# Cutting GpSimd's attention multiplies into four pieces, and a shorter run of rank operations

## The chip, the cores and the metric

The kernel runs on one core of a Trainium2 chip, in one launch. The metric is the device time of one execution in microseconds (us), the median of the runs. Engines are called as in the profile: PE (TensorE), DVE (VectorE), ACT (ScalarE), POOL (GpSimd), SP (the queue that issues most DMAs).

## The reference, cut to what matters

```python
kv  = einsum('bhsd,bhse->bhde', k, v)              # 4 batches, 8 heads, 576 positions, 64 wide
out = einsum('bhsd,bhde->bhse', q, kv)
out = out / sqrt(mean(out*out, -1) + 1e-6) * g_norm
x   = out.transpose(0, 2, 1, 3).reshape(2304, 512)  # 2304 tokens = 18 tiles of 128
# first mixture: tokens with x @ w_skip > 0 go to expert argmax(x @ w_gate), 8 experts, 512->1024->512
y   = gate * (relu(x @ w1[e]) @ w2[e]);  x[chosen] += y
# second mixture: all tokens, other weights, capacity 576 an expert
out[i] = gate * (relu(x[i] @ w1[e]) @ w2[e])
```

## The kernel before, in words

**Attention.** Tokens are worked off in 18 tiles of 128 (`emit_tile`, L734). For a tile PE multiplies q with the batch's kv matrix into PSUM (`emit_products`, L730); the same product carries 34 more columns per head pair, from which the tile's 17 logits come. ACT squares the result (L739), DVE sums the squares per head (L741), ACT copies the result out of PSUM as `og` (L747; DVE does so for tile 15) and takes the root (L749), DVE takes its reciprocal `ri` (L751) and forms the logits in `Lall` (L755, L757). POOL then does two multiplies over 128 x 512 elements at L762: `og` by the norm weights, in place, and `xr` = `og` by `ri`. SP stores `xr` to the token table `xcat` in HBM (L765), one DMA a tile, in SP's order.

**Routing.** While the tiles run, the chosen experts are made into one-hots and ranks in two parts, tiles 0 to 8 and tiles 9 to 17. `onehot_all` (L148) is six DVE operations over (tiles x 8 experts). `rank_part` (L167) makes running counts `C` on DVE (L173), lets PE sum them over partitions (L178 to L183), and turns ranks `rk` into a block number `hb` (L200, L202), a place in the block `a` (L204), block one-hots `os` (L207), their product with the experts `Bt` (L214), and per tile a 128 x 128 one-hot `As` of the place (L218), all on DVE. PE multiplies `As` with `Bt` (L794, L855), which gives each slot's token number. In the second part the total of the counts, `sum`, is one small POOL addition (L188); PE's matmul L260 in `order_experts` takes `sum`, and its result is what DVE sorts the experts by. The call for the first mixture has two blocks (`nb` = 2), that for the second three.

**An early start.** After the first part the largest expert is known. Its first 128 tokens are gathered by POOL (`gather`, L339) as soon as their numbers are there (`tokens`, L271 to L273), and SP loads its weights (L329). PE starts on them (L574, L592) while the second part of the routing is finished.

**What sets the order.** PE's order is written out by hand in `ATT_SEQ` and `EARLY_SEQ`; the part of it around the change is "v7 t v3 h0 h1 R h2 h3 T y0 y1": fill-in matmuls, transposes `t` of the gathered rows, the hidden blocks `h0`, `h1`, then `R` (the rank matmuls L178 to L183 and L260), `h2`, `h3`, then `T` (L855). DVE, ACT, POOL and SP run their instructions in the order that a planner gave them, by priority (the program's order, with `late` parts behind) and by its own costs; each engine then runs strictly in that order. POOL's order in this stretch is: the multiplies of the tiles, the gather in the midst of them, and last the copy of the one-hots (L677) and `sum` (L188).

Of the kernel before, what the change touches and what calls it, by code (L numbers as in the profile page):

```python
# [11 lines left out]
ALU = mybir.AluOpType  # L12
# [5 lines left out]
B, H, S, HD = 4, 8, 576, 64  # L18
# [13 lines left out]
EPS_G = 1e-9  # L32
LPOOL = 16
G_DVE = (15,)
EARLY_SEQ = "v7 t v3 h0 h1 R h2 h3 T y0 y1"
ATT_SEQ = ["t0 c0 c1 t1 t2 c2 c3 c4 t3 T", "t0 c0 c1 t1 t2 c2 c3 c4 t3 T t4", "r t0 q c0 c1 t1 t2 c2 c3 R c4 t3 T", "e m0 m1 E w w p0 p1 t2 w w t3 t4"]
KV_COL = True
# [5 lines left out]
def blocks(n):  # L43
    return [(r, min(128, n - r)) for r in range(0, n, 128)]
# [3 lines left out]
def moe_kernel(ctx: ExitStack, tc: tile.TileContext, qT, kk, vv, aux, w1a, w2a, w1b, w2b, capacity, out):  # L48
    nc = tc.nc
# [29 lines left out]
    pi100 = cst.tile([128, NT, 2], F32, name="pi100")  # L79
# [63 lines left out]
    def behind(inst, other):  # L143

        tc.add_manual_dep(inst.ins, other.ins.name, mybir.DependencyInfo(mybir.DependencyClass.NoSync, mybir.DependencyReason.SCHED_ONLY),
                          reason="what waits for other comes first")
# [17 lines left out]
    ahead = {}  # L164
    As = rt.tile([128, NT, 128], BF16, name="As")

    def rank_part(st, ohv, i0, i1, ps_pool, tag, base=None, bump=None):  # L167

        m, nb = st["m"], st["nb"]
        n = i1 - i0  # L170
        nm = lambda s: f"{s}_{m}_{i0}"
        C = rt.tile([128, E, n], BF16, name=nm("C"))
        nc.vector.tensor_tensor_scan(out=C.rearrange("p e i -> p (e i)"), data0=smask[n].rearrange("p e i -> p (e i)"),  # L173
                                     data1=ohv.rearrange("p e i -> p (e i)"), initial=0.0, op0=ALU.mult, op1=ALU.add)
        yield
        R = ps_pool.tile([128, E, n], F32, name=tag)
        prev = st["sum"]
        nc.tensor.matmul(R, lhsT=ones, rhs=C, start=True, stop=False)  # L178
        if prev is not None:
            nc.tensor.matmul(R, lhsT=ones, rhs=prev.unsqueeze(2).to_broadcast([128, E, n]), start=False, stop=False)  # L180
        if bump is not None:
            nc.tensor.matmul(R, lhsT=identb, rhs=bump.unsqueeze(2).to_broadcast([128, E, n]), start=False, stop=False)
        nc.tensor.matmul(R, lhsT=ntri, rhs=ohv, start=False, stop=True)  # L183
        if prev is None:
            st["sum"] = C[:, :, n - 1]
        else:
            st["sum"] = rt.tile([128, E], BF16, name=nm("sum"))
            ins = nc.gpsimd.tensor_tensor(out=st["sum"], in0=prev, in1=C[:, :, n - 1], op=ALU.add)  # L188
            if m == 1 and bump is not None:
                behind(ins, ahead["gather"])  # L190
        if i1 == NT and m == 1:
            order_experts(st, ps_pool, tag)
        rk8 = rt.tile([128, E, n], F32, name=nm("rk8"))
        if base is not None:
            nc.vector.tensor_tensor(out=rk8, in0=R, in1=base.unsqueeze(2).to_broadcast([128, E, n]), op=ALU.add)
        nc.vector.tensor_tensor(out=rk8, in0=R if base is None else rk8, in1=ohv, op=ALU.mult)
        rk = rt.tile([128, n], F32, name=nm("rk"))
        nc.vector.tensor_reduce(out=rk, in_=rk8.rearrange("p e i -> p i e"), axis=AX.X, op=ALU.add)
        hb = rt.tile([128, n], F32, name=nm("hb"))
        nc.vector.tensor_scalar(out=hb, in0=rk, scalar1=128.0, scalar2=None, op0=ALU.is_ge)  # L200
        for k in range(2, nb + 1):
            nc.vector.scalar_tensor_tensor(out=hb, in0=rk, scalar=128.0 * k, in1=hb, op0=ALU.is_ge, op1=ALU.add)  # L202
        a = rt.tile([128, n], F32, name=nm("a"))
        nc.vector.scalar_tensor_tensor(out=a, in0=hb, scalar=-128.0, in1=rk, op0=ALU.mult, op1=ALU.add)  # L204
        os_ = rt.tile([128, n, 2, nb], BF16, name=nm("os"))
        for k in range(nb):
            nc.vector.scalar_tensor_tensor(out=os_[:, :, :, k], in0=hb.unsqueeze(2).to_broadcast([128, n, 2]), scalar=float(k),  # L207
                                           in1=pi100[:, i0:i1, :], op0=ALU.is_equal, op1=ALU.mult)
        x2 = 2 * nb
        Bt = st["Bt"]  # L210
        step = 6 if n == NT else n
        for h0 in range(0, n, step):
            hs = slice(h0, h0 + step)
            nc.vector.tensor_tensor(out=Bt[:, i0 + h0:i0 + h0 + step], in0=ohv[:, :, hs].rearrange("p e i -> p i e").unsqueeze(3).to_broadcast([128, step, E, x2]),  # L214
                                    in1=os_[:, hs].rearrange("p i q b -> p i (q b)").unsqueeze(2).to_broadcast([128, step, E, x2]), op=ALU.mult)
            for i in range(h0, h0 + step):
                eng = nc.gpsimd if m == 1 and i1 == NT and i < AS_POOL else nc.vector
                eng.tensor_scalar(out=As[:, i0 + i, :], in0=rowb, scalar1=a[:, i:i + 1], scalar2=None, op0=ALU.is_equal)  # L218
# [37 lines left out]
    def order_experts(st, ps_pool, tag):  # L256

        m = st["m"]
        cps = ps_pool.tile([128, E], F32, name=tag)
        nc.tensor.matmul(cps, lhsT=ones, rhs=st["sum"], start=True, stop=True)  # L260
        key = rt.tile([128, E], F32, name=f"key_{m}")
        nc.vector.tensor_tensor(out=key, in0=cps, in1=st["head"], op=ALU.add)
        sort_experts(st, key)
        cnt0 = rt.tile([1, E], F32, name=f"cnt0_{m}")
        nc.scalar.copy(out=cnt0, in_=cps[0:1])
        st.update(ends=cnt0)
# [370 lines left out]
    with att:  # L637
# [96 lines left out]
        def emit_tile(i):  # L734
            if i not in PS:
                emit_products(i)
            ps, t0 = PS[i], i * 128
            sq = asp.tile([128, 4, 128], F32, name="sq")
            nc.scalar.activation(out=sq, in_=ps[:, :, 0:128], func=AF.Square)  # L739
            ss = asp.tile([128, H], F32, name="ss")  # L740
            nc.vector.tensor_reduce(out=ss, in_=sq.rearrange("p c (h d) -> p (c h) d", h=2), axis=AX.X, op=ALU.add)  # L741
            og = aog.tile([128, H, HD], F32, name="og")
            o4, og4 = ps[:, :, 0:128].rearrange("p c (h d) -> p c h d", h=2), og.rearrange("p (c h) d -> p c h d", c=4)
            if i in G_DVE:
                nc.vector.tensor_tensor(out=og4, in0=o4, in1=grep.unsqueeze(1).unsqueeze(1).to_broadcast([128, 4, 2, HD]), op=ALU.mult)
            else:
                nc.scalar.copy(out=og4, in_=o4)  # L747
            rm = asp.tile([128, H], F32, name="rm")
            nc.scalar.activation(out=rm, in_=ss, func=AF.Sqrt, bias=eps6, scale=1.0 / HD)  # L749
            ri = asp.tile([128, H], F32, name="ri")  # L750
            nc.vector.reciprocal(out=ri, in_=rm)  # L751
            xr = axp.tile([128, ROW], F32, name="xr")
            r4 = ri.rearrange("p (c h) -> p c h", c=4).unsqueeze(3)
            lh = asp.tile([128, 4, 2, 17], F32, name="lh")
            nc.vector.tensor_tensor(out=lh, in0=ps[:, :, 128:162].rearrange("p c (h n) -> p c h n", h=2),  # L755
                                    in1=r4.to_broadcast([128, 4, 2, 17]), op=ALU.mult)
            nc.vector.tensor_reduce(out=Lall[:, i, :], in_=lh.rearrange("p c h n -> p n (c h)"), axis=AX.X, op=ALU.add)  # L757
            (nc.gpsimd.tensor_copy if i >= LPOOL else nc.scalar.copy)(out=xr[:, D:ROW], in_=Lall[:, i, 0:16])
            steps = [] if i in G_DVE else [(og, grep.unsqueeze(1))]
            steps.append((xr[:, 0:D].rearrange("p (h d) -> p h d", h=H), ri.unsqueeze(2)))  # L760
            for k, (dst, by) in enumerate(steps):
                ins = nc.gpsimd.tensor_tensor(out=dst, in0=og, in1=by.to_broadcast([128, H, HD]), op=ALU.mult)  # L762
                if "gather" in ahead and k == 0 and i > ahead["first"]:
                    behind(ins, ahead["gather"])
            nc.sync.dma_start(out=xcat[t0:t0 + 128, :], in_=xr)  # L765

        with tc.manual_schedule(engines={mybir.EngineType.PE}):
# [74 lines left out]
            with tc.tile_pool(name="e1t", bufs=2, space=PSUM, reuse_waits="tile") as p1t, \  # L842
                    tc.tile_pool(name="e1h", bufs=2, space=PSUM, reuse_waits="tile") as p1h, \
                    tc.tile_pool(name="e1y", bufs=2, space=PSUM, reuse_waits="tile") as p1y:
                for u in EARLY_SEQ.split():
                    if u == "t":
# [22 lines left out]
    with first_mix:  # L869
# [288 lines left out]
        step = tc.manual_schedule(engines={mybir.EngineType.PE})  # L1158
# [100 lines left out]
    with tc.tile_pool(name="m2y", bufs=1) as m2y, tc.tile_pool(name="m2o", bufs=4) as m2o, \  # L1259
# [85 lines left out]
        for p, j in enumerate(ORDER2):  # L1345
# [16 lines left out]
            nb = len(blocks(CAP2[j]))  # L1362
# [61 lines left out]
```

## Time and profile before

| | us |
|---|---|
| runs: median (lowest to highest of 3) | 495.9 (495.35 to 496.73) |
| the profiled execution, its own time | 496.99 |
| its span in the trace | 495.3 |

The span is the time from the first to the last instruction of the trace; the profiled execution took 1.7 us more than its span, which lies around it. In the rows below, times are us from the span's start, durations us unless marked ns. "L762" is line 762 of the program. In a timeline row the first number is the start, the second the duration (of several instructions together where "x2" stands), and in brackets the idle time of the engine just before and what ended it.

### The profile page before, as it was taken

How to read it: one execution, taken by the hardware profiler on the slowest of the kernel's cores; microseconds unless marked ns; L12 is line 12 of the kernel's file. 1: busy time of each engine (PE TensorE's matmuls, PEld its weight loads, DVE VectorE, ACT ScalarE, POOL GpSimd, SP SyncE). 2: the span in 40 equal slices, each digit the busy share in tenths (PEclk: the TensorE clock that was granted, in tenths of full speed). 3: DMA queues.
4: the chain of work that ended last, by engine and by line, in shares of the span. 5: the costliest groups of instructions: out<-in, count | busy, mean ns of one | idle time of the engine just before them, and what ended most of it. 6: DMA issues, size and time to landing. Idle time of an engine off the chain costs nothing.

```text
span 495.3 us, 10229 instructions
## 1 busy us (share of the span) xinstructions
PE 472.4 (95%) x3829; PEld 450.1 (91%) x3829; DVE 303.6 (61%) x942; ACT 205.3 (41%) x524; POOL 146.5 (30%) x179
## 2 busy tenths in 40 slices
PE   6998689999999999999998999999999999999995
PEld 3897578999999999999897899999999999999984
DVE  2157988568766775356774576565657566675711
ACT  1376451354352532106143364454545545555400
POOL 5288684104112032022123240220604124040201
PEclk9599999999999999999999999999999999999999
DMA  8999495998868676259119983554656656300001
GB/s 244 367 360 343 166 356 145 359 357 313 293 216 284 228 246 235 97 195 346 60 47 343 396 293 140 201 189 154 212 185 221 204 174 216 148 37 1 36 23 41
DMA packets 24617, 104.90 MB, mean 212 GB/s; under 512 B 3609, under 2 KB 4761, under 8 KB 15984
## 3 DMA queue, kind: packets, MB, share of 16 engines
q1 hardware_dynamic: 17264, 77.75, 45.6%
q0 software_dynamic: 7008, 26.35, 15.2%
q8 instruction: 32, 0.52, 0.4%
q14 instruction: 25, 0.20, 0.1%
q10 hardware_dynamic: 288, 0.07, 0.1%
HBM read 92.15 MB, written 12.76 MB: 212 GB/s over the span
## 4 chain that ended last, share of the span: by engine, by line
PE 75%; DVE 4%; DMA 2%; issue 1%; ACT 0%; POOL 0%; POOLq 0%; ACTq 0%
PE hp L592 14%; PE yp L1086 7%; PE yp L1088 7%; PE yp L1087 7%; PE hp L1086 6%; PE yp L616 6%; PE hp L1087 6%; PE hp L1088 6%; PE yp L626 5%; PE yp L617 2%; PE yt L1317 2%; DMA wraw<-in_w1b 2%; PE tp L1273 2%; PE tp L1010 1%; PE tp L574 1%; DVE wlo L979 1%
## 5 line engine op out<-in xcount | busy, mean ns | idle before, releaser
L978 ACT CAST whi<-wraw 128x512 fp32r<-128x512 f32 x152 | 86.1, 619 | 75.0 <-PE yp L1087 30.1
L979 DVE TENSOR_TENSOR wlo<-wraw,whi 128x512 fp32r<-128x512 f32 x152 | 97.3, 685 | 28.9 <-ACT whi L978 27.8
L339 POOL DMA_INDIRECT rows<-xcat,gi x40 | 42.6, 1064 | 137.3 <-ACT ex L348 86.0
L1086 PE MATMUL hp<-xh,whi 128*128 128x256 f32 (+7 forms) x256 | 78.9, 308 | 0.2 <-DVE hl L1106 0.2
L592 PE MATMUL hp<-xT,wraw 128*128 128x128 f32 (+8 forms) x576 | 78.0, 292 | 0.3 <-issue 0.3
L1088 PE MATMUL hp<-xh,wlo 128*128 128x256 f32 (+7 forms) x256 | 76.6, 299 | 0.0
L1087 PE MATMUL hp<-xl,whi 128*128 128x256 f32 (+7 forms) x256 | 76.6, 299 | 0.0
L592 PEld LDWEIGHTS hp<-xT,wraw 128*128 128x128 f32 x576 | 73.4, 190 | 2.5 <-issue 2.4
L1307 POOL DMA_INDIRECT out<-ot,toki x24 | 34.6, 1444 | 85.4 <-DVE su L352 39.4
L1086 PE MATMUL yp<-hh,whi 128*128 128x320 f32 (+5 forms) x192 | 58.8, 306 | 0.0
L1087 PE MATMUL yp<-hl,whi 128*128 128x320 f32 (+5 forms) x192 | 57.3, 298 | 0.0
L1088 PE MATMUL yp<-hh,wlo 128*128 128x320 f32 (+5 forms) x192 | 57.2, 298 | 0.0
L1086 PEld LDWEIGHTS hp<-xh,whi 128*128 128x128 f32 x256 | 48.2, 188 | 1.0 <-DVE hl L1106 0.7
L1087 PEld LDWEIGHTS hp<-xl,whi 128*128 128x128 f32 x256 | 48.4, 189 | 0.0
L1088 PEld LDWEIGHTS hp<-xh,wlo 128*128 128x128 f32 x256 | 48.2, 188 | 0.0
L1026 POOL DMA_INDIRECT xcat<-rows,toki x16 | 16.4, 1026 | 92.5 <-DVE mxt L297 90.0
L616 PE MATMUL yp<-hT,whi 128*128 128x352 f32 (+4 forms) x160 | 43.1, 351 | 0.0
L1105 ACT ACTIVATE hh<-hp 128x320 fp32r<-128x320 f32 (+8 forms) x64 | 27.2, 429 | 32.2 <-PE hp L1088 27.4
L1106 DVE SCALAR_TENSOR_TENSOR hl<-hp,hh 128x320 fp32r<-128x320 f32 (+8 forms) x64 | 30.1, 477 | 13.5 <-ACT hh L1105 12.3
L617 PE MATMUL yp<-hT,wlo 128*128 128x176 f32 (+4 forms) x160 | 37.8, 236 | 0.0
L1087 PEld LDWEIGHTS yp<-hl,whi 128*128 128x128 f32 x192 | 36.2, 188 | 0.0
L1086 PEld LDWEIGHTS yp<-hh,whi 128*128 128x128 f32 x192 | 36.1, 188 | 0.0
(253 smaller groups left out, 866.6 us busy)
## 6 DMA issues: line engine op xcount, KB each, us to landing
wraw<-in_w1a SPq DMA_DIRECT2D x14, 1024.0 KB
wraw<-in_w2a SPq DMA_DIRECT2D x14, 1024.0 KB
wraw<-in_w1b SPq DMA_DIRECT2D x14, 1024.0 KB
wraw<-in_w2b SPq DMA_DIRECT2D x14, 1024.0 KB
xcat<-xr SPq DMA_DIRECT2D x18, 264.0 KB
q<-in_q SPq DMA_DIRECT2D x3, 1152.0 KB
wraw<-in_k SPq DMA_DIRECT2D x6, 512.0 KB
wraw<-in_v SPq DMA_DIRECT2D x6, 512.0 KB
```

The costliest lines, as they stand in the source:

```text
L339: return nc.gpsimd.indirect_dma_start(out=rows[:n], out_offset=None, in_=xcat[0:source], in_offset=bass.IndirectOffsetOnAxis(ap=gi[:n], ax ...
L592: nc.tensor.matmul(hp[:, ff, :], lhsT=wv[:, fc % 4, k, :], rhs=XT[j][:, k, c0:c1], start=(k == 0), stop=(k == 3))
L616: nc.tensor.matmul(yp, lhsT=wh[:, fc, :], rhs=HT[j][:, fc], start=(fc == 0), stop=False, skip_group_check=True)
L617: nc.tensor.matmul(yp[:, 0, :], lhsT=wl[:, fc, :], rhs=HT[j][:, fc, 0, :], start=False, stop=(fc == 7), skip_group_check=True)
L978: nc.scalar.copy(out=hi[:, cs], in_=raw[:, cs])
L979: ins = nc.vector.tensor_tensor(out=lo[:, cs], in0=raw[:, cs], in1=hi[:, cs].bitcast(F32), op=ALU.subtract)
L1086: nc.tensor.matmul(ps, lhsT=wh, rhs=xh, start=first, stop=False)
L1087: nc.tensor.matmul(ps, lhsT=wh, rhs=xl, start=False, stop=False)
L1088: nc.tensor.matmul(ps, lhsT=wl, rhs=xh, start=False, stop=last)
L1105: ea = nc.scalar.activation(out=hh[:, fs, cs], in_=hp, func=AF.Relu)
L1106: ev = nc.vector.scalar_tensor_tensor(out=hl[:, fs, cs], in0=hp, scalar=0.0, in1=hh[:, fs, cs].bitcast(F32), op0=ALU.max, op1=ALU.subtract)
L1307: st = nc.gpsimd.indirect_dma_start(out=out, out_offset=bass.IndirectOffsetOnAxis(ap=r2["toki"][:nn, j, bi:bi + 1], axis=0), in_=ot[:nn], ...
```

## The change

From tile 7 on (the eighth) each POOL multiply of 128 x 512 elements is issued as four instructions of 128 x 128, two heads each. In `rank_part`, with two blocks, `hb` becomes minus 128 or 0 in one operation, `a` is the sum of `hb` and `rk`, and the two `os` one-hots compare `rk` with 128 directly: four DVE operations where there were five, and `os` no longer reads `hb`. With three blocks nothing changes. `rank_part` runs with two blocks twice.

```diff
+PIECES = (7, 4)
...
-        nc.vector.tensor_scalar(out=hb, in0=rk, scalar1=128.0, scalar2=None, op0=ALU.is_ge)
-        for k in range(2, nb + 1):
-            nc.vector.scalar_tensor_tensor(out=hb, in0=rk, scalar=128.0 * k, in1=hb, op0=ALU.is_ge, op1=ALU.add)
...
-        nc.vector.scalar_tensor_tensor(out=a, in0=hb, scalar=-128.0, in1=rk, op0=ALU.mult, op1=ALU.add)
...
-        for k in range(nb):
-            nc.vector.scalar_tensor_tensor(out=os_[:, :, :, k], in0=hb.unsqueeze(2).to_broadcast([128, n, 2]), scalar=float(k),
-                                           in1=pi100[:, i0:i1, :], op0=ALU.is_equal, op1=ALU.mult)
+        if nb == 2:
+            nc.vector.tensor_scalar(out=hb, in0=rk, scalar1=128.0, scalar2=-128.0, op0=ALU.is_ge, op1=ALU.mult)
+            nc.vector.tensor_tensor(out=a, in0=hb, in1=rk, op=ALU.add)
+            for k, op in enumerate((ALU.is_lt, ALU.is_ge)):
+                nc.vector.scalar_tensor_tensor(out=os_[:, :, :, k], in0=rk.unsqueeze(2).to_broadcast([128, n, 2]), scalar=128.0,
+                                               in1=pi100[:, i0:i1, :], op0=op, op1=ALU.mult)
+        else:
...
             for k, (dst, by) in enumerate(steps):
-                ins = nc.gpsimd.tensor_tensor(out=dst, in0=og, in1=by.to_broadcast([128, H, HD]), op=ALU.mult)
-                if "gather" in ahead and k == 0 and i > ahead["first"]:
-                    behind(ins, ahead["gather"])
+                by = by.to_broadcast([128, H, HD])
+                step = H if i < PIECES[0] else H // PIECES[1]
+                for h0 in range(0, H, step):
+                    hs = slice(h0, h0 + step)
+                    ins = nc.gpsimd.tensor_tensor(out=dst[:, hs], in0=og[:, hs], in1=by[:, hs], op=ALU.mult)
+                    if "gather" in ahead and k == 0 and i > ahead["first"]:
+                        behind(ins, ahead["gather"])
```

## Rows read from the trace of the kernel before

**Rows 1.** The page: busy time of the engines over the span.

```profile
PE 472.4 (95%) x3829; PEld 450.1 (91%) x3829; DVE 303.6 (61%) x942; ACT 205.3 (41%) x524; POOL 146.5 (30%) x179
```

**Rows 2.** The chain of waits, 0 to 95 us, first piece: start, us, what.

```profile
82.41 0.34 issue
```

**Rows 3.** The timeline of PE, 48 to 78 us.

```profile
48.09 0.19 PE L178 MATMUL lg<-C,ones 128*128 128x72 bf16 x1 [1.80 <-DVE C L173]
...
59.73 0.35 PE L794 MATMUL acc<-Bt,As 128*128 128x32 bf16 x2 [1.31 <-DVE As L218]
...
68.41 0.63 PE L574 MATMUL tp<-ident,rows 128*128 128x128 f32 x4 [1.74 <-DMA rows<-xcat,gi]
...
73.72 0.18 PE L260 MATMUL lg<-sum,ones 128*128 128x8 bf16 x1 [0.33 <-DVE rk L196]
73.82 3.81 PE L592 MATMUL hp<-xT,wraw 128*128 128x128 f32 x32
```

**Rows 4.** Stretches: length, PE, PEld, DVE, ACT, POOL busy; PE clock; DMA.

```profile
39.70:72.90 33.20, 25.73 (x236) 22.39 (x235) 29.83 (x89) 18.14 (x50) 26.08 (x28) 0.95 0.81 283
44.30:62.00 17.70, 12.07 (x123) 10.56 (x122) 17.38 (x58) 8.56 (x24) 11.65 (x12) 0.96 0.65 225
56.00:60.00 4.00, 1.01 (x11) 0.56 (x9) 4.00 (x17) 2.12 (x6) 2.30 (x2) 1.00 0.17 68
61.00:63.00 2.00, 2.00 (x9) 2.00 (x9) 1.94 (x7) 0.20 (x1) 1.50 (x2) 0.50 0.97 377
```

**Rows 5.** DVE, single lines: duration ns least/median/most, first and last start.

```profile
L157 DVE TENSOR_TENSOR oa_eq<-Lall,oa_mx x3: 309/630/968, 44.7 to 81.5; 128x72 f32<-128x72 f32 x2, 128x144 f32<-128x144 f32 x1
...
L200 DVE TENSOR_SCALAR hb<-rk x3: 168/171/1033, 50.8 to 92.5; 128x9 f32<-128x9 f32 x2, 128x18 f32<-128x18 f32 x1
...
L202 DVE SCALAR_TENSOR_TENSOR hb<-rk,hb x4: 160/178/961, 51.8 to 92.9; 128x9 f32<-128x9 f32 x2, 128x18 f32<-128x18 f32 x2
...
L204 DVE SCALAR_TENSOR_TENSOR a<-hb,rk x3: 160/178/1191, 52.8 to 93.1; 128x9 f32<-128x9 f32 x2, 128x18 f32<-128x18 f32 x1
...
L533 DVE TENSOR_SCALAR lead_1l<-key_1l,mx_1l x1: 890/890/890, 56.4 to 56.4; 128x8 f32<-128x8 f32 x1
...
L218 DVE TENSOR_SCALAR As<-rowb,a x36: 232/251/916, 54.1 to 97.4; 128x128 bf16<-128x128 bf16 x36
...
L271 DVE SCALAR_TENSOR_TENSOR tok<-tab x6: 159/162/940, 60.9 to 255.6; 128x1 f32<-128x1 f32 x3, 128x14 f32<-128x14 f32 x1, 128x2 f32<-128x2 f32 x1, 128x21 f32<-128x21 f32 x1
```

**Rows 6.** The timeline of POOL, 0 to 73 us.

```profile
2.00 0.58 POOL L100 MEMSET capc<- 1x1 f32 x16
...
8.57 4.08 POOL L964 TENSOR_SCALAR inslot<-pcol 128x1 f32<-128x1 f32 x16
...
39.70 1.26 POOL L762 TENSOR_TENSOR og<-og,au 128x512 f32<-128x512 f32 x1
...
42.07 2.49 POOL L762 TENSOR_TENSOR og<-og,au 128x512 f32<-128x512 f32 x2
44.52 2.05 POOL L762 TENSOR_TENSOR xr<-og,ri 128x512 f32<-128x512 f32 x2
...
60.76 1.04 POOL L762 TENSOR_TENSOR xr<-og,ri 128x512 f32<-128x512 f32 x1 [1.13 <-issue]
62.30 1.29 POOL L339 DMA_INDIRECT rows<-xcat,gi  x1 [0.50 <-DVE gi L272]
...
70.42 0.20 POOL L758 COPY xr<-Lall 128x16 f32<-128x16 f32 x1
70.59 1.03 POOL L762 TENSOR_TENSOR xr<-og,ri 128x512 f32<-128x512 f32 x1
...
72.65 0.21 POOL L188 TENSOR_TENSOR sum<-C,C 128x8 bf16<-128x8 bf16 x1
```

**Rows 7.** The timeline of SP's queue, 51 to 60 us.

```profile
51.81 6.37 SPq L765 DMA_DIRECT2D xcat<-xr  x3
59.05 0.90 SPq L329 DMA_DIRECT2D wraw<-in_w1a  x2
```

More of the change, by code (lines that the diff above doesn't have):

```diff
@@ L199, in rank_part @@
         hb = rt.tile([128, n], F32, name=nm("hb"))
-        nc.vector.tensor_scalar(out=hb, in0=rk, scalar1=128.0, scalar2=None, op0=ALU.is_ge)
-        for k in range(2, nb + 1):
-            nc.vector.scalar_tensor_tensor(out=hb, in0=rk, scalar=128.0 * k, in1=hb, op0=ALU.is_ge, op1=ALU.add)
         a = rt.tile([128, n], F32, name=nm("a"))
-        nc.vector.scalar_tensor_tensor(out=a, in0=hb, scalar=-128.0, in1=rk, op0=ALU.mult, op1=ALU.add)
         os_ = rt.tile([128, n, 2, nb], BF16, name=nm("os"))
-        for k in range(nb):
-            nc.vector.scalar_tensor_tensor(out=os_[:, :, :, k], in0=hb.unsqueeze(2).to_broadcast([128, n, 2]), scalar=float(k),
-                                           in1=pi100[:, i0:i1, :], op0=ALU.is_equal, op1=ALU.mult)
+        if nb == 2:
[5 more added lines that the diff above has]
+        else:
+            nc.vector.tensor_scalar(out=hb, in0=rk, scalar1=128.0, scalar2=None, op0=ALU.is_ge)
+            for k in range(2, nb + 1):
+                nc.vector.scalar_tensor_tensor(out=hb, in0=rk, scalar=128.0 * k, in1=hb, op0=ALU.is_ge, op1=ALU.add)
+            nc.vector.scalar_tensor_tensor(out=a, in0=hb, scalar=-128.0, in1=rk, op0=ALU.mult, op1=ALU.add)
+            for k in range(nb):
+                nc.vector.scalar_tensor_tensor(out=os_[:, :, :, k], in0=hb.unsqueeze(2).to_broadcast([128, n, 2]), scalar=float(k),
+                                               in1=pi100[:, i0:i1, :], op0=ALU.is_equal, op1=ALU.mult)
         x2 = 2 * nb
```

## The prediction

> **What bounds the kernel now.** I read the page first: PE is busy 95% of the span [rows 1], so any time that PE loses comes out at the end. The chain of waits, read from its start, begins only at 82.41 us [rows 2]; from there on it is nearly all PE, so what a change before 82 us is worth is how much earlier or later PE gets there, and the timeline of PE between 48 and 78 us is the view that decides. It shows four waits: 1.80 us for the counts `C` of DVE, 1.31 us for `As` of DVE, 1.74 us for the gathered rows, 0.33 us ahead of L260 [rows 3]. From L260 at 73.72 us on PE has matmuls back to back until the chain of waits takes over [rows 3].
>
> The first three waits lead to DVE: of the 17.70 us from 44.3 to 62.0 it is busy 17.38 [rows 4], and the gather at 62.30 waits for its `gi` [rows 6]. DVE is slow there because it meets POOL. The first L157 starts at 44.7 and takes 0.97 us, ending at 45.66; the first of two `xr` multiplies that start at 44.52 ends half-way through their 2.05 us, at 45.55 [rows 5, 6]. With POOL idle the same operation on twice the elements takes 0.31 [rows 5]. So a DVE operation that reads two operands from SBUF, or a small tensor_scalar, stands until the POOL multiply that it met is over, and gets in ahead of the next one. POOL itself is busy 26.08 of the 33.20 us from 39.7, where tile 7's multiplies start, to 72.9, just behind `sum` (72.65 + 0.21 = 72.86) [rows 4, 6]: 7.1 us idle.
>
> **The change part by part. DVE's gain.** Eight stalls on DVE's way to the gather, long minus short duration [rows 5]: L157 and the operation after it, 0.97 - 0.23 each (0.23 is an estimate from half of 0.31 and the fixed part of the others): 1.48; L200 1.03 - 0.17: 0.86; L202, which goes: 0.96; L204 1.19 - 0.16: 1.03; L533 0.89 - 0.17 (L200's short form stands in): 0.72; the worst `As` 0.92 - 0.25: 0.67; L271 0.94 - 0.16: 0.78. Sum 6.5 us. With pieces, the seven that stay still wait for a piece, at most 0.42 us long (below); I take half, 0.2 each: 1.4 back. POOL will also have few gaps left, so the operations that fell into its gaps until now (two `os`, `Bt`, half of the nine `As`, three small ones of the lead expert, some 11) wait 0.2 us each: 2.2 back. Net 6.5 - 1.4 - 2.2 = 2.9 us; bounds 6.5 (no waits left) and 6.5 - 18 x 0.42 = -1.1. The dropped operation of the second `rank_part` saves 0.16 us [rows 5], ahead of `T`, which PE reaches behind h3 in any case: nothing.
>
> **POOL's price.** 21 multiplies (10 by the norm weights, since tile 15's is on DVE, and 11 by `ri`) become 84. No row before shows a 128 x 128 multiply on POOL, so I work it out from starts, not durations. A multiply by the weights takes 1.26 us alone and two take 2.49, so one follows another after 1.23; by `ri` 2.05 - 1.04 = 1.01 [rows 6]. Their small end: `sum`, the same operation on 8 elements, takes 0.21, and with the 0.03 by which neighbours overlap that is 0.17 to 0.18; the copy of 16 elements at 70.42 is followed at 70.59, after 0.17 [rows 6]. Through 0.17 at 8 and 1.23 at 512 elements a straight line gives 0.42 at 128, four of them 1.69: +0.46. By `ri`: 0.37, four 1.48: +0.47. Sum 10 x 0.46 + 11 x 0.47 = 9.8 us. From both sides: a fixed part f costs 63 f. The cheapest small row is the memset, 0.58/16 = 0.036 (2.3 us in all), the dearest the tensor_scalar, 4.08/16 = 0.255 (16.1 us) [rows 6]. I take f of some 0.155, that of the same operation and of the copy, which agree.
>
> POOL's order puts `sum` behind all of these multiplies, and they start at 39.70 as before, since the work up to there is untouched. DVE running earlier can only take out POOL's idle time, 7.1 us. So `sum` ends no sooner than 72.86 + 9.8 - 7.1 = 75.6. L260 needs it, and PE is in order: behind L260 stand h2, h3, `T` and all that follows. L260 then starts at about 75.7 instead of 73.72: **+2.0 us**. The early gather lies in POOL's order behind tile 13's `xr`, 14 multiplies into the stretch: 39.70 + 7 x (1.69 + 1.48) + 0.35 for the one-hot copy = 62.2, about its 62.30 of now, so DVE's gain doesn't reach the rows either; if the planner puts the gather ahead of tile 13's pieces, h0 and h1 start earlier and PE only waits longer at L260. Two further steps lie beside this wait. SP's weight loads at 59.05 stand behind the store of tile 12 [rows 7]; with POOL behind, that `xr` ends at 39.70 + 6 x 3.17 + 0.35 = 59.1 and the loads go out about a microsecond later, so h0 and h1 end about 74.3, still ahead of 75.7. From L260 on everything moves together (the sort on DVE waits for its result as PE's h2 does), and nothing behind it makes up for the loss, PE being the chain. The added instructions wait for `og` as one did, and DVE delaying single pieces, at 0 to 1.5 us in all, is left to the range.
>
> The profiled execution took 496.99 us, 1.1 above the median of the runs: its span 495.3 + 1.7. With +2.0 it would take 499.0, and the median 495.9 + 2.0 = **497.9**.
>
> The rows put f at 0.155 from two places. [...]
>
> **The rivals.** (a) Pieces are cheap, and DVE's gain passes. With f up to 0.08 the added 5.0 us stay within the 7.1 idle plus the 0.75 us that `sum` has in hand at L260 (73.72 - 72.86, less 0.1 for the signal), the gather comes 2.9 us sooner, and so do the rows, `C`, `sum` and L260: 495.9 - 2.9 = 493.0. For it: DVE has no other slack in the stretch; against it: POOL's small instructions, none of which but the memset starts its follower in under 0.17. It decides from f = 0.125 downwards (7.85/63). (b) The two cancel: f between 0.10 and 0.15, L260 within 1.5 us of now: 495.9. [...] (d) The dearer fixed part, 0.2: 12.6 added, 500.7.
>
> **How the numbers follow.** Forecast 0.44, with 496.4 to 500.0 as its own range (f from 0.13 to 0.19); (a) 0.27; (b) 0.15; (c) 0.09; (d) 0.05. 0.3%, 1.5 us, is about what a measurement of this kernel can tell from no change. Faster by more: (a) nearly whole, 0.26. Within: (b) and the lower end of the forecast, 0.24. Slower by more: 0.50. The range from 493.0 to 500.5 leaves the better half of (a) below and (d) above, 0.17 in all.
>
> **What the profile after would show.** Right: `og` and `xr` pieces follow one another after 0.37 to 0.43 us, POOL has almost no idle time from 39.7 to the gather and on to `sum`, `sum` ends at 75 us or later, PE idles ahead of L260 with POOL as what ended it, and no DVE operation there takes over 0.6 us. Wrong: pieces 0.35 us apart or less, `sum` done well ahead of h1's end, the gather before 60. My figures fall if the planner puts `sum` ahead of the last pieces, or if POOL's idle time can't be used because pieces wait for ACT; then only the first half, DVE's gain, or only the second is seen.

## The result and the profile after

The changed kernel takes 500.44 us (median of four runs, 500.04 to 503.38) against 495.75 for the kernel before in the same comparison: 4.7 us longer by the medians; over all runs the ratio is 1.0105, with a 95% interval of 1.0063 to 1.0146. The forecast was 497.9, so the sign was right and the size was not. The profiled execution took 500.69 us with a span of 499.0, 3.7 us more than before. Line numbers have moved by 1 to 12: L158 is the comparison that was L157, L774 the multiplies, L179 the rank matmuls, L268 the matmul that takes `sum`.

The page, busy time of each engine: POOL has 63 instructions and 8.9 us more [rows 1], DVE two instructions fewer and yet 4.6 us more.

```profile
PE 474.8 (95%) x3824; PEld 452.6 (91%) x3829; DVE 308.2 (62%) x940; ACT 205.4 (41%) x524; POOL 155.4 (31%) x242
```

The timeline of PE (start, duration, and in brackets the idle time before it with what ended it):

```profile
50.99 0.22 PE L179 MATMUL lg<-C,ones 128*128 128x72 bf16 x1 [4.51 <-DVE C L174]
...
71.40 1.09 PE L582 MATMUL tp<-ident,rows 128*128 128x128 f32 x4 [4.24 <-DMA rows<-xcat,gi]
...
73.56 4.13 PE L600 MATMUL hp<-xT,wraw 128*128 128x128 f32 x32
78.48 0.21 PE L179 MATMUL lg<-C,ones 128*128 128x72 bf16 x1 [0.79 <-DVE C L174]
79.11 0.18 PE L268 MATMUL lg<-sum,ones 128*128 128x8 bf16 x1 [0.33 <-DVE rk L197]
```

The wait for `C` has grown from 1.80 to 4.51 us, that for the rows from 1.74 to 4.24, and L268 starts 5.39 us later than L260 did [rows 3]. `C` comes from DVE, and the rows come late because POOL, which issues their gather, had stood for DVE before. DVE's timeline shows why:

```profile
44.59 0.37 DVE L765 TENSOR_REDUCE Lall<-lh 128x17 f32<-128x136 f32 x1
44.88 4.41 DVE L158 TENSOR_TENSOR oa_eq<-Lall,oa_mx 128x72 f32<-128x72 f32 x1
49.33 0.23 DVE L159 TENSOR_TENSOR oa_eq<-oa_eq,w 128x72 f32<-128x72 f32 x1
...
53.76 0.81 DVE L207 SCALAR_TENSOR_TENSOR os<-rk,pi 128x18 bf16<-128x18 f32 x2
54.49 0.43 DVE L205 TENSOR_TENSOR a<-hb,rk 128x9 f32<-128x9 f32 x1
...
70.33 6.43 DVE L158 TENSOR_TENSOR oa_eq<-Lall,oa_mx 128x72 f32<-128x72 f32 x1
76.80 0.23 DVE L159 TENSOR_TENSOR oa_eq<-oa_eq,w 128x72 f32<-128x72 f32 x1
```

The first comparison of each part, over 128 x 72 elements, takes 4.41 and 6.43 us; before it took 0.97 and 0.63 [rows 5]. At 53.76 and 54.49, `os` and `a` take some 0.4 us each: these got in at the end of a piece, as forecast. POOL's timeline shows what the comparisons stood for:

```profile
39.90 1.69 POOL L774 TENSOR_TENSOR og<-og,au 128x128 f32<-128x128 f32 x4
41.55 1.47 POOL L774 TENSOR_TENSOR xr<-og,ri 128x128 f32<-128x128 f32 x4
42.99 2.52 POOL L774 TENSOR_TENSOR og<-og,au 128x128 f32<-128x128 f32 x6
...
47.73 1.46 POOL L774 TENSOR_TENSOR xr<-og,ri 128x128 f32<-128x128 f32 x4
50.66 0.33 POOL L685 COPY OH<-oh 128x72 bf16<-128x72 bf16 x1 [1.47 <-DVE oh L162]
...
75.21 1.46 POOL L774 TENSOR_TENSOR xr<-og,ri 128x128 f32<-128x128 f32 x4
76.63 0.19 POOL L766 COPY xr<-Lall 128x16 f32<-128x16 f32 x1
78.14 0.33 POOL L685 COPY OH<-oh 128x72 bf16<-128x72 bf16 x1 [1.32 <-DVE oh L162]
78.50 0.21 POOL L189 TENSOR_TENSOR sum<-C,C 128x8 bf16<-128x8 bf16 x1
```

The first comparison ends at 49.29; POOL's last piece ahead of the copy of `OH` ended at 47.73 + 1.46 = 49.19. The second ends at 76.76; POOL's last piece ends at 75.21 + 1.46 = 76.67. So neither comparison stood for one piece. Each stood until POOL stopped, and POOL stopped only because its next instruction, the copy, needs the one-hots that hang on this very comparison: POOL then waits 1.47 and 1.32 us for DVE, on top.

### The profile page after: what moved, and what is told of

It is laid out like the page before. It is cut to its first block, busy times and chain, and to the rows that moved or that the text cites. A ratio compares the mean times of both kernels' runs of the same rounds, so it can differ in the third digit from the quotient of the medians.

```text
span 499.0 us, 10286 instructions
## 1 busy us (share of the span) xinstructions
PE 474.8 (95%) x3824; PEld 452.6 (91%) x3829; DVE 308.2 (62%) x940; ACT 205.4 (41%) x524; POOL 155.4 (31%) x242
## 4 chain that ended last, share of the span: by engine, by line
PE 77%; DVE 3%; DMA 1%; issue 0%; ACT 0%; POOL 0%; POOLq 0%; ACTq 0%
PE hp L600 14%; PE yp L1098 7%; PE yp L1100 7%; PE yp L1099 7%; PE hp L1098 6%; PE hp L1099 6%; PE hp L1100 6%; PE yp L624 6%; PE yp L634 5%; PE yp L625 2%; PE tp L1285 2%; PE yt L1329 2%; PE tp L1022 1%; PE tp L582 1%; DMA rows<-xcat,gi 1%; PE lg L1009 1%
```

## The experiments

The question is why a comparison of DVE stands behind a whole run of POOL's pieces while `os` and `a` stand behind one. Theories A and B are told in the first expectation. Times are compared with the kernel before on the same chip.

**The stall by itself.** A kernel with none of the computation, executed once: 23 stretches of POOL multiplies, most of them 20 of 128 x 128, and beside each stretch one DVE operation run twice, in other sizes and forms.

```diff
+        for c in range(count):
...
+            ins = nc.gpsimd.tensor_tensor(out=d, in0=s, in1=b.to_broadcast([128, h, 64]), op=ALU.mult)
...
+        go = nc.vector.tensor_reduce(out=st, in_=flag, axis=AX.X, op=ALU.max)
...
+        for z in "xy":
...
+            ins = test(r)
```

> This kernel leaves the whole computation out: POOL runs stretches of back-to-back multiplies (mostly 20 of 128x128 f32, some of 256, 512 and 64 columns, two with a memset after each), and in each stretch DVE runs one two-input or tensor_scalar operation twice. Theory A (a DVE operation of the kind of the first one-hot comparison, 72 f32 elements with one operand repeated along the row, is not let in between 128-column pieces and stands until POOL pauses): that form takes over 5 us, until its stretch of some 8 us ends, while 9 or 18 elements take 0.2 to 0.5 us. Which of size, operand order, repeated operand or number type decides shows from the forms beside it. Rival B (it is let in at the next piece's end, as the prediction had it, and the 4.4 and 6.4 us in the changed kernel had another cause): every form takes 0.2 to 0.6 us with 128-column pieces, and up to 1.4 us with 512 columns.

No multiply of a stretch depends on another; `test` is the DVE operation. Its groups for one form, a DVE multiply over 9, 18, 36, 72 and 144 elements, the first run of each (least/median/most duration in ns, then start):

```profile
L81 DVE TENSOR_TENSOR rdax<-big x1: 437/437/437, 4.9 to 4.9; 128x9 f32<-128x9 f32 x1
...
L81 DVE TENSOR_TENSOR rdbx<-big x1: 8149/8149/8149, 12.9 to 12.9; 128x18 f32<-128x18 f32 x1
...
L81 DVE TENSOR_TENSOR rdcx<-big x1: 354/354/354, 21.5 to 21.5; 128x36 f32<-128x36 f32 x1
...
L81 DVE TENSOR_TENSOR rddx<-big x1: 8203/8203/8203, 29.9 to 29.9; 128x72 f32<-128x72 f32 x1
...
L81 DVE TENSOR_TENSOR rdex<-big x1: 467/467/467, 38.6 to 38.6; 128x144 f32<-128x144 f32 x1
```

Neither theory survives: 18 and 72 elements stand 8.2 us, to the end of the stretch ("locked"), and 9, 36 and 144 do not ("open"). The same alternation goes on through the other forms of 128 columns, up to the stretch of 256. What alternates is POOL's history. After a stretch in which DVE was locked out, POOL's next instruction had to wait for it (0.2 us ahead of the stretch with 36 elements, 0.3 ahead of that with 144), and the stretch behind this pause was open. There DVE got through early, POOL ran into the next stretch without a pause, and that one was locked. Hence theory A2: after an unbroken run of POOL instructions DVE is no longer let in at their ends, until POOL pauses.

Two of the last stretches don't fit A2 as it stands. That of 64 columns was open (0.26 us) though POOL had not paused since 156.68; DVE had got in at 166.53, in the stretch ahead. And a stretch with a memset behind every multiply locked (7.26 us), but let DVE in at 188.43 while POOL ran on without a wait.

**One half alone: the rank operations.** The multiplies stay whole.

```diff
-PIECES = (7, 4)
+PIECES = (18, 4)
```

> Multiplies whole as before, only the shorter rank operations stay. Theory A and rival B: one stalled operation fewer on DVE's way to the early gather, about 1 us earlier there: 494.5 to 495.9. Rival C (the loss is from the rewritten rank operations): 497 or more.

496.35 us, ratio 1.0022 (0.9995 to 1.0048): nothing gained or lost. The comparisons take 0.96 and 1.03 us, L179 waits 1.80 us for `C` as before; the stalls of the operations that went moved on to the two `os` (1.11 us together, 0.26 in the kernel before) and `Bt` (1.48, before 0.45). The microsecond that was expected did not come.

**The other half alone: the pieces.** The rank operations are those of before.

```diff
-        if nb == 2:
...
-        else:
+        nc.vector.tensor_scalar(out=hb, in0=rk, scalar1=128.0, scalar2=None, op0=ALU.is_ge)
```

> Pieces from tile 7 on, rank operations as before the change. Theory A: the first comparison of each part again takes 4 us or more, C is 5 us late at the second rank matmuls, 500 to 501.5. Rival C: 495 to 497.

501.38 us, ratio 1.0107 (1.0066 to 1.0148), comparisons of 4.38 and 6.34 us: the pieces alone make a loss of the same size.

**Pieces only where no comparison waits.** Tiles 10 to 13 in four, the others whole.

```diff
-PIECES = (7, 4)
+PIECES = (10, 11, 12, 13)
...
-                step = H if i < PIECES[0] else H // PIECES[1]
+                step = H // 4 if i in PIECES else H
```

> Pieces for tiles 10 to 13 alone, which are multiplied between the two one-hot comparisons; tiles 7 to 9 and 14 to 17 whole; rank operations as changed. Theory A: both comparisons take about 1 us as before, the operations between them lose their 1 us stalls (0.4 us each), the gather goes out 1 to 2.5 us earlier than in the kernel before, and the time is 493.5 to 495. Rival B (POOL's own length is what costs): 8 multiplies cost 3.8 us of POOL, within its 7 us of idle time, so about 495.5; theory A and B part at the comparisons' durations.

498.85 us, ratio 1.0055 (1.0031 to 1.0079). The comparisons are short again (0.97 and 0.24), the gather starts at 60.44 instead of 62.30 and the rows come to PE at 67.23 instead of 68.41 (some 0.6 us of this lies ahead of the pieces: tile 7's first multiply starts at 39.10 here and at 39.70 before); yet L268 starts at 74.17, later than the 73.72 of before, and the 493.5 to 495 that were expected did not come. PE had idled 4.13 us for the rows, and then

```profile
69.00:71.00 2.00, 2.00 (x12) 2.00 (x11) 1.40 (x2) 0.83 (x2) 1.44 (x4) 0.50 0.97 356
```

(a stretch, with busy us of PE, PEld, DVE, ACT and POOL, then the granted clock: 0.50). The earlier rows were there, and PE ran the work behind them at a clock of 0.50.

**How long a run.** Again none of the computation, and one execution: one comparison of DVE, started by the n-th multiply since POOL last paused.

```diff
+            s = part(dst, c - 1) if chain and c and c % chain == 0 else part(big, c)
...
+            ins = nc.gpsimd.tensor_tensor(out=d, in0=s, in1=b.to_broadcast([128, h, 64]), op=ALU.mult)
...
+            ins = nc.vector.tensor_reduce(out=st, in_=part(dst, a - 1)[:, 0:8], axis=AX.X, op=ALU.max)
...
+            go = nc.vector.tensor_tensor(out=r.rearrange("p (i e) -> p i e", e=8), in0=wide[:, 0:9, 0:8],
+                                         in1=col[:, 0:9].unsqueeze(2).to_broadcast([128, 9, 8]), op=ALU.is_equal)
```

> Leaves the whole computation out: POOL runs stretches of multiplies that each begin after a pause of POOL; in each the DVE comparison (72 f32 elements, the form of the first comparison of the one-hots) arrives after n multiplies of the stretch. Theory A2 (DVE gets in at a multiply's end only while few multiplies have followed one another unbroken since POOL last paused; after a long run it is locked out until POOL pauses): short (0.25 to 0.5 us) for small n, 4 us or more (the rest of the stretch) from some n between 8 and 20 on with 128 columns; a multiply that has to wait for the one ahead of it (each 4th reads what the one ahead wrote) brings it back in; five comparisons spread over one stretch all get in. Rival D (no count matters, only the form or chance): long and short mixed over n, and the waits change nothing.

With `chain` every multiply whose number it divides reads the result of the one ahead; the small reduction of the `a`-th multiply's result starts the comparison. DVE's timeline; the rows stand for n = 13, n = 16, n = 17 where every fourth multiply reads the result of the one ahead, and the last of five comparisons at 4, 8, 12, 16 and 20:

```profile
65.89 0.39 DVE L92 TENSOR_TENSOR ragzm<-wide,col 128x72 f32<-128x72 f32 x1
...
78.73 5.76 DVE L92 TENSOR_TENSOR rahzp<-wide,col 128x72 f32<-128x72 f32 x1
...
264.39 0.39 DVE L92 TENSOR_TENSOR rcdzq<-wide,col 128x72 f32<-128x72 f32 x1
...
292.85 0.39 DVE L92 TENSOR_TENSOR rcfzt<-wide,col 128x72 f32<-128x72 f32 x1
```

After 1 to 13 pieces the comparison takes 0.39 us, after 16 and after 20 it takes 5.76, to the end of the stretch. Where every fourth multiply has to wait for the one ahead of it, it takes 0.39 at the 17th. Five comparisons spread over 20 multiplies are all let in. With 256 columns no run up to 10 multiplies locked (0.66 us each), with 512 none up to 8 (1.20 us). A2 holds in its first half: a long unbroken run locks, a short one does not, and for these pieces the border lies between 13 and 16. But the run is not counted from POOL's last pause alone: the last of the five comparisons came 20 multiplies behind it and got in. It fits, and so does the 64-column stretch, that a DVE operation let in also begins the count anew; that is a reading, no trace shows a count.

The kernel has such breaks too. In the kernel before, a whole `xr` multiply reads the `og` that the one just ahead writes:

```profile
41.04 1.04 POOL L762 TENSOR_TENSOR xr<-og,ri 128x512 f32<-128x512 f32 x1
```

It starts 0.08 us after that one's end (39.70 + 1.26 = 40.96), and three multiplies had ended since when the first comparison started at 44.69. Cut in four, the first `ri` piece reads an `og` piece that lies three pieces back, and follows the fourth without a break (41.55 behind 39.90 + 1.69): 16 multiplies had ended since POOL's last wait, at 35.43, when the first comparison started.

**The clock in the middle variant.** The kernel of the mid tiles with 20 fill-in matmuls instead of 7 ahead of the transposes.

```diff
-EARLY_SEQ = "v7 t v3 h0 h1 R h2 h3 T y0 y1"
+EARLY_SEQ = "v20 t v3 h0 h1 R h2 h3 T y0 y1"
```

> The kernel with pieces for tiles 10 to 13 alone, and 20 instead of 7 fill-in matmuls on PE ahead of the transposes of the gathered rows. In the run without them PE idled 4.1 us there, its clock then stood at 0.50, and the 1.2 us that the rows came earlier were lost again. Theory: with PE kept busy the clock stays at 1.00, the second rank matmuls come 1 to 1.7 us sooner than in that run, and the time is 1 to 2 us below it and 0 to 1.5 us below the kernel before. Rival (the fill-in delays the transposes, or the clock falls all the same): no better than the run without.

495.9 us, ratio 0.9989 (0.9964 to 1.0014). The same stretch as above, now with the clock at 1.00:

```profile
69.00:71.00 2.00, 2.00 (x19) 1.97 (x18) 1.93 (x3) 1.61 (x3) 1.75 (x4) 1.00 0.98 312
```

L268 starts at 73.34 instead of 74.17. With the fill-in the clock stays at 1.00 and the loss is gone; but with the clock at 1.00 the pieces of these four tiles are worth nothing measurable: the rows still land at 68.03.

**A pause in POOL's run, with all pieces kept.** The four `ri` pieces of a tile in reversed order, so that the first reads the `og` piece just ahead of it and must wait for it.

```diff
-                for h0 in range(0, H, step):
+                for h0 in range(0, H, step)[::-1 if k == len(steps) - 1 else 1]:
```

> The changed kernel with the four pieces of each multiply by ri issued from the last heads to the first, so that the first of them waits for the piece of og just written: as many instructions and as much work, with a pause of some 0.1 us of POOL at some of them. Theory A2: DVE gets in again, both first comparisons take 0.6 us or less (4.4 and 6.4 us in the changed kernel), C of the first part is ready by 48 us, PE waits for no 4 us there, and the time falls by 2 us or more from the changed kernel's, to 496 to 498.5; what is left above the kernel before is POOL's own length, which the prediction put at 2.0 us, with L268 waiting for sum. Rival D (chance): comparisons of 4 us or more, 500 or more.

498.56 us, ratio 1.0059 (1.0041 to 1.0077). The first comparison takes 0.26 us and the wait for `C` shrinks to 0.97; the second stands 6.42 us as in the changed kernel, because no piece waited there: POOL's timeline has no gap between the gather and the end of the pieces. The planner had moved other pieces between the `og` piece and the one that reads it (tile 14's third `ri` piece ahead of its fourth, a piece of tile 17 between tile 16's `og` and `xr`). L268 starts at 77.16 instead of 79.11. One of the two lock-outs is gone, and the ratio is 1.0059 instead of 1.0105, though the two intervals overlap.

**Two pieces.**

```diff
-PIECES = (7, 4)
+PIECES = (7, 2)
```

> The changed kernel with two pieces a multiply instead of four: half as many instructions in a run, 21 added instead of 63, 3.3 us of POOL. Theory A2 (a run of 13 still lets DVE in, one of 16 doesn't; some 12 stand ahead of the first comparison here): comparisons 0.7 us, C a little earlier than before the change, 494.5 to 496.5. If the number of instructions doesn't matter and the time of unbroken work does: comparisons of 4 us or more, 499 or more.

495.70 us, ratio 0.9997 (0.9977 to 1.0017). The first comparison takes 0.68, the second 3.88 us, to the end of POOL's run. Ten multiplies had run since the last wait of POOL, and the early gather among them; after ten of this size without a gather the comparison got in, in 0.66 us, in the kernel of runs alone. A count of 13 to 16 is therefore not the whole rule; whether the gather counts for more than a multiply was not tried alone.

**Pieces by tile.** Two for tiles 8 and 9, four for 10 to 13, whole from 14 on, and 20 fill-in matmuls.

```diff
-PIECES = (7, 4)
+PIECES = {8: 2, 9: 2, 10: 4, 11: 4, 12: 4, 13: 4}
...
-                step = H if i < PIECES[0] else H // PIECES[1]
+                step = H // PIECES.get(i, 1)
```

> Two pieces for tiles 8 and 9, four for tiles 10 to 13, whole multiplies elsewhere, and 20 fill-in matmuls. Theory A2: no comparison over 1 us, the early gather by 60 us, PE's clock at 1.00 ahead of h0; but the rows land with the DMA engines full, so only a part of the 2 us or more at the gather shows: 494 to 495.8, against some 496 for the kernel before. If the gather's lead counts in full: under 494.

495.05 us, ratio 0.9977 (0.9962 to 0.9992): 1.1 us ahead of the kernel before by the ratio, 0.6 by the medians; little, but the interval excludes none. The comparisons take 0.70 and 0.24 us, L268 starts at 73.75. No run has the 20 fill-in matmuls with whole multiplies, so it is not shown that the pieces made this gain.

**All pieces, a pause in both parts.** The reversed order, and from tile 15 on every multiply of POOL held behind the one ahead of it in the program, so that tiles 14 to 17 go in order. What is left of the loss should then be POOL's own length, the term that the forecast rested on.

```diff
+                    if i > 14:
+                        behind(ins, ahead["mul"])
+                    ahead["mul"] = ins
```

> The changed kernel with the four ri pieces of a tile in reversed order of heads and, from tile 14 on, POOL's multiplies held to the tiles' order, so that each tile's first ri piece comes right behind the norm-weight piece that it reads and has to wait for it; all pieces are still there. Theory A2 (what shuts DVE's comparison out is an unbroken run of POOL pieces, some 14 or more): both comparisons of onehot_all take under 0.9 us, C no longer ends last, and POOL's own length, which the prediction worked out, is what is left: POOL idle under 0.6 us ahead of the copy OH, sum ends at 75.2 to 75.9 us, PE's L268 starts at 75.3 to 76.2 (73.72 before), time +1.2 to +2.0: 497.0 to 497.8. Rival D (the gather itself, or POOL's total load, shuts DVE out, whatever the waits): the second comparison again stands over 3 us, to the last ri piece; sum behind it at 76.5, L268 at 77, time 498.5 as with the reversed pieces alone.

497.65 us (496.84 to 499.17), ratio 1.0048 (1.0030 to 1.0066), 1.8 us above the kernel before beside it. POOL's timeline at the end of the stretch:

```profile
68.15 1.68 POOL L774 TENSOR_TENSOR og<-og,au 128x128 f32<-128x128 f32 x4
69.91 1.47 POOL L774 TENSOR_TENSOR xr<-og,ri 128x128 f32<-128x128 f32 x4
...
74.79 0.25 POOL L685 COPY OH<-oh 128x72 bf16<-128x72 bf16 x1
74.98 0.21 POOL L189 TENSOR_TENSOR sum<-C,C 128x8 bf16<-128x8 bf16 x1
```

and DVE's, the first and the second comparison:

```profile
44.64 0.41 DVE L158 TENSOR_TENSOR oa_eq<-Lall,oa_mx 128x72 f32<-128x72 f32 x1
...
68.15 1.77 DVE L158 TENSOR_TENSOR oa_eq<-Lall,oa_mx 128x72 f32<-128x72 f32 x1
```

The second misses the expected 0.9 and says most: locked out from 68.15, it ends at 69.92. POOL's `og` pieces end at 68.15 + 1.68 = 69.83 and the `xr` piece that must wait for the last of them starts at 69.91. DVE got in at the first break in POOL's run, 0.08 us wide, with 12 multiplies still to come. The rival (the gather or POOL's load shuts DVE out whatever the waits) falls; that the gather helps a run to lock, as the run with two pieces hints, does not. POOL no longer waits for `oh`, and `sum` ends at 75.19 us. L268 starts at 76.20, at the upper end of what was expected, and not for `sum`, as PE's timeline shows:

```profile
69.25 0.63 PE L582 MATMUL tp<-ident,rows 128*128 128x128 f32 x4 [3.89 <-DMA rows<-xcat,gi]
...
70.63 5.11 PE L600 MATMUL hp<-xT,wraw 128*128 128x128 f32 x32
75.57 0.20 PE L179 MATMUL lg<-C,ones 128*128 128x72 bf16 x1
```

After 3.89 us of idling for the rows the 32 matmuls of h0 and h1 take 5.11 us (3.73 in the kernel before); the granted clock is 0.57 from 70 to 74. POOL's length and the low clock come out 1.0 us apart here, the clock last.

**The same with more fill-in.** 20 fill-in matmuls.

> The kernel of e8_both_free with 20 fill-in matmuls instead of 7 ahead of the transposes. If POOL's length sets L268, more fill-in changes L268 by less than 0.4 us (75.3 to 76.2) and the time by what the clock gives back in h0 and h1 only if these end after sum: 496.5 to 497.8, clock 1.00 in 69 to 74. If instead the low clock of the gathered rows' wait is what is left, L268 comes at 73.5 and the time is 495.5.

497.86 us, ratio 1.0039 (1.0018 to 1.0061): neither branch. PE still idles 2.79 us ahead of the rows, the clock falls to 0.50 from 72 to 74, L268 comes at 76.53. Whether `sum` alone would have held L268 at 75.3 could not be shown.

**The same with two pieces.** `PIECES = (7, 2)`.

> The kernel of e9_both_free_warm with two pieces to a multiply. The fixed part is then paid 21 times instead of 63: +3.3 us, less than POOL's idle time, so sum is no longer the last: both comparisons under 0.9 us (Theory A2), sum ends by 72.5, L268 at 73.2 to 73.8, time 494.5 to 495.5 (0.1 to 0.2% under the kernel before). Rival D: second comparison 3.9 us as in e6_two_pieces, L268 at 74.3, 495.7.

494.88 us, ratio 0.9984 (0.9967 to 1.0001), on the border of a gain. The comparisons take 0.39 and 0.37 us, `sum` ends at 71.64, L268 starts at 72.88, 0.84 us earlier than L260 did. With pauses, two pieces and 20 fill-in matmuls, splitting does no harm; what the fill-in would give by itself was not tried here either.

## Why the prediction was right in sign and wrong in size

**The step that failed** is in DVE's gain: "With pieces, the seven that stay still wait for a piece, at most 0.42 us long". It was read off the kernel before, where a DVE operation "stands until the POOL multiply that it met is over, and gets in ahead of the next one". That held for whole multiplies, and in the changed kernel it holds for `os`, `a` and `As` (some 0.4 us each) and for `Bt` (0.78, where it took 0.45 before). It failed for the two comparisons, which met POOL after an unbroken run of pieces. Four times as many instructions between two waits of POOL, and the lost break between a tile's `og` and its `xr`, made such runs, and no row of before had one. So DVE's term, forecast as 2.9 us gained at the gather with -1.1 as its worst end, was a loss: on DVE the first comparison costs 4.41 - 0.97 = 3.4 us more and the second 6.43 - 0.63 = 5.8.

PE pays for them otherwise than these two numbers suggest. Its timeline before, between the rows' arrival and L260 [rows 3]:

```profile
69.52 3.73 PE L592 MATMUL hp<-xT,wraw 128*128 128x128 f32 x32
73.09 0.20 PE L178 MATMUL lg<-C,ones 128*128 128x72 bf16 x1
```

Beside the rows of after: of the 5.39 us by which L268 is late, 2.99 are there when the gathered rows arrive (71.40 against 68.41), which goes back to the first lock-out. From the rows to the 32 matmuls are 2.16 us where there were 1.11, and from there to the rank matmuls 4.92 where there were 3.57; these 2.40 us more are the clock of 0.50, shown below, and 0.79 of waiting for `C`. So the second comparison, the dearer one on DVE, stops PE for 0.79 us, since it stands while PE still waits for the rows and works on them.

That one DVE instruction waits for one of POOL's is what the 0.4 us rows show. The 4.41 and 6.43 us rows go further: DVE waited through more than ten instructions. What in the chip makes a run lock was not shown.

**POOL's price was nearly right.** 1.69 and 1.48 us were forecast for four pieces, from one start to the next. The starts lie 1.65 apart for four weight pieces (39.90 to 41.55) and 1.44 for four `ri` pieces (41.55 to 42.99), so the pieces add 10 x 0.42 + 11 x 0.43 = 8.9 us where 9.8 were forecast: a fixed part f of 0.14. That is above the 0.08 of the rival with cheap pieces (a), a value that no row or run shows, and below the 0.2 of the dear one (d); both are out by it, and that (d)'s 500.7 lies beside the measured 500.44 is luck. (The 0.1 that (a) takes for the signal was an estimate too: L260 starts 0.06 us behind the DVE operation that it waits for in the kernel before, at 73.72 behind 73.43 + 0.23.) It fits the forecast's 0.13 to 0.19, and also the 0.10 to 0.15 of (b). The last `xr` ends at 76.67, past the forecast bound of 75.6, but POOL's wait of 1.47 us for the first comparison is in that. And `sum` was not what L268 waited for: POOL ended its pieces and then waited 1.32 us for `oh`. With both lock-outs broken `sum` ends at 75.19, within 0.5 us of the forecast 75.6, and the time, 497.65, is within 0.3 us of the forecast 497.9. That agreement is partly luck, since there the clock, 1.0 us behind `sum`, sets L268.

**The gather did not stay.** It was to lie at about 62.2 and lies at 64.50:

```profile
60.98 1.70 POOL L774 TENSOR_TENSOR og<-og,au 128x128 f32<-128x128 f32 x4 [0.46 <-ACT og L755]
62.85 1.48 POOL L774 TENSOR_TENSOR xr<-og,ri 128x128 f32<-128x128 f32 x4 [0.18 <-POOL og L774]
64.50 1.30 POOL L347 DMA_INDIRECT rows<-xcat,gi  x1 [0.17 <-DVE Lall L765]
```

That it hangs in POOL's order behind tile 13's `xr`, as forecast, held: `gi` was done at 63.11, and the gather stood until that `xr` ended at 64.33. What the sum lacked is POOL's idle time ahead of it, above all the 1.47 us that the copy of `OH` waits for the first comparison; with the lock-outs broken the gather lies at 62.33. The weight loads, forecast a microsecond later than 59.05 [rows 7], go out at 61.64 in the changed kernel and at 60.09 with the lock-outs broken.

**The clock fell as well, the rival (c), but at another place.** The 498.9 of (c) is the forecast and 1.0 us more, an estimate of the author's for h2 at a clock of 0.50, which the kernel before shows from 61 to 63 us [rows 4]; no run shows that term. In the changed kernel PE idles 4.51 and 4.24 us, and some time behind each of the two waits a stretch has the clock at 0.50:

```profile
53.00:56.00 3.00, 2.78 (x11) 2.41 (x12) 3.00 (x11) 1.65 (x5) 3.00 (x9) 0.50 0.34 127
66.00:71.00 5.00, 1.15 (x6) 0.31 (x4) 4.65 (x14) 2.66 (x8) 5.00 (x14) 1.00 0.94 363
71.00:73.00 2.00, 1.60 (x6) 1.15 (x7) 2.00 (x1) 0.83 (x3) 2.00 (x6) 0.50 0.97 243
```

It did not fall at h2, behind a wait at L260, but at the transposes and first matmuls behind the wait for the rows.

**"Nothing behind it makes up for the loss" was wrong by a third.** L268 is 5.39 us late, the span only 3.7. The stretch from 200 to 300 us, first in the kernel before:

```profile
200.00:300.00 100.00, 97.74 (x763) 91.69 (x762) 60.04 (x212) 36.05 (x91) 25.83 (x25) 1.00 0.61 220
```

and the kernel after:

```profile
200.00:300.00 100.00, 99.51 (x794) 93.63 (x793) 61.39 (x220) 35.05 (x89) 26.80 (x28) 1.00 0.62 226
```

PE idles 2.26 us of this before and 0.49 after. The chain of waits of before has a transfer there that the delay hides, the next weights:

```profile
260.44 9.06 DMA wraw<-in_w1b
```

After, this piece is not on the chain; a gather of rows stands there with 4.99 us. So 1.8 of the 5.4 us were given back. The load itself moved with the rest: POOL issues it at 260.44 before and at 266.19 after, 5.75 us later. But ACT, which waits for it, starts on it only 3.79 us later:

```profile
269.58 1.14 ACT L978 CAST whi<-wraw 128x512 fp32r<-128x512 f32 x2 [7.04 <-DMA wraw<-in_w1b]
...
273.37 1.14 ACT L990 CAST whi<-wraw 128x512 fp32r<-128x512 f32 x2 [5.10 <-DMA wraw<-in_w1b]
```

The first row is of before, the second of after. From issue to use it took 9.1 us and then 7.2; why it was faster is not shown.

**What the profile after was to show**: the end of `sum` past 75 us and the loss came out, the spacing of the pieces nearly (0.41 and 0.36 us, where 0.37 to 0.43 were forecast); "almost no POOL idle time", POOL as the ender ahead of L260 and "no DVE operation over 0.6 us" did not, and the last of these three is the sign that names the failed step.

## What to carry to other kernels

Splitting an instruction to let a neighbour in can shut it out, as it did here (4.41 and 6.43 us for 0.97 and 0.63): how long one instruction is was not all that counted, but also how many ran without a wait (13 pieces of 128 columns let DVE in after 0.39 us, 16 did not). Before splitting, look in the timeline for what makes the other engine pause, and keep a pause inside each stretch that the neighbour must enter (here a dependency on the instruction just ahead, 0.08 us, did). And not all of a loss need arrive at the end: here 1.8 of 5.4 us came back at a later load, so look on the chain for transfers behind the change before forecasting that all of it is paid.

## What the runs showed of the hardware that was not expected

- DVE's comparison over 128 x 72 elements got in at the end of a POOL multiply after short runs (0.39 us at up to 13 of 128 columns) and stood to the end of the run after long ones (5.76 us at 16); a `tensor_scalar` over 128 x 72 f32 elements was locked out as well (8.17 us). A pause of 0.08 us between two dependent POOL instructions was enough to let DVE in, and after letting DVE in a run went on without locking (five comparisons over 20 multiplies, 0.39 us each). What in the chip counts the run was not seen in any trace, and the border is open: ten multiplies of 256 columns with a gather among them locked (3.88 us), ten without one did not.
- Memsets between POOL's multiplies did not keep the run open: the comparison beside such a stretch stood 7.26 us. Yet it got in at 188.43 us, with POOL still at work and no wait of POOL's in sight; why it got in there is not shown.
- POOL's multiply showed a fixed part of about 0.14 us: by the norm weights four quarters took 1.69 us and two halves 1.41 against 1.26 for the whole [rows 6], which is 0.43 for three more instructions and 0.15 for one. The forecast's estimate of 0.155 was close, and 63 times 0.14 is 8.8 us, close to the 8.9 more on the page.
